# Loading q and k of the first four groups as eight tokens per row, and transposing them by quarter products

## The chip, the cores and the metric

The kernel runs on one core of one Trainium2 chip. The metric is the device time of one launch in microseconds; each figure of a kernel is the median of several runs. TensorE (PE in the profile, PEld for its weight loads) multiplies matrices into PSUM; VectorE (DVE), ScalarE (ACT) and GpSimd (POOL) do the work in between, POOL without PSUM. SyncE (SP) issues all DMAs of this kernel, in the order of its one queue.

## What is computed

Attention within chunks of 64 tokens, then two feed-forward layers on 4608 tokens of width 512. The inputs q, k, v are 8 x 8 x 576 x 64 (batch, head, token, dimension) in float32; the weights come as float64.

```python
scores = matmul(q_c, k_c.transpose(0, 1, 2, 4, 3)) / sqrt(64)     # by chunks of 64 tokens
attn = exp(scores - max(scores)); attn = attn / (sum(attn) + 1e-9)
x = matmul(attn, v_c)                          # -> x: 4608 tokens x 512
h = x @ w_in;  x = relu(h)**2 @ w_out          # 512 -> 2048 -> 512
h = x @ w_in2                                  # second layer
P = a[0] + a[1]*h + a[2]*h**2 + a[3]*h**3
Q = 1 + |b[0]|*|h| + |b[1]|*h**2
out = (P / (Q + 1e-6)) @ w_out2
```

## The kernel before

The work is cut into 36 tiles of 128 tokens and 9 blocks of 512. Products of the two layers are made in three matmuls each, of a high and a low float32r half of both operands (mm3, lines 265 to 269). A block takes 16 steps s: mm_h makes 128 columns of h, act1 squares and splits them, mm_out1 adds them into four accumulators. While the first layer of block b runs, DVE, ACT and POOL make the attention of later tiles, and the weights of the first layer are loaded, made into float32 and split: w_load (DMA), w_words (two instructions on ACT), w_join (DVE), w_split (a cast, then a subtraction on POOL that gives the low half).

The order is written out by hand. Each step is put at a time by `at`, with a correction from the table MOVED; ON says which engine does a copy, a cast or a norm, or how many dummy transposes of the identity (warm) stand at a place. `issue` sorts by time, and the program order of every engine follows from it. So the tables set the order of instructions and not a start: an instruction starts when its engine reaches it and its semaphores allow it.

The change is about block 0, whose 512 tokens are handled as four groups g: 256 tokens of four heads each. For a group, load_group loads q, k or v (tiles qs, ks: two buffers each, by the group's parity; v0, v1, vx0, vx1), g_tr transposes q or k on PE (steps tq, tk), g_copy brings the result from PSUM to SBUF (qc, kc). Then come the scores g_s (step s), max, sub, exp, sum, norm, the transposition of the result g_f (f), its copy (cp), the product with v (pv) and the split of x into two halves (xh, xl). The list `order` in line 819 holds these steps together with words, join and split of the first two weights and the first six half products (half000 is step 0, tokens 0 to 255, first half of the sum). The loads before them stand in the list of line 791. Tiles 4 and 5 follow as whole tiles (tr_second, line 427; mm_s, line 452; f_tr, line 650), and later tiles come by another path with DVE transposes.

In the loop of g_tr a 128 x 128 piece holds 128 tokens of two heads, so a group's q takes four transpositions, and head 2p+h of the group stands in partition half h of column block p:

Of the kernel before, what the change touches and what calls it, by code (L numbers as in the profile page):

```python
# [9 lines left out]
F32 = mybir.dt.float32  # L10
# [13 lines left out]
LN_SHIFT = 20  # L24
ON = {
# [12 lines left out]
MOVED = {  # L38
# [37 lines left out]


@with_exitstack
def attn_moe_moe_kernel(
# [25 lines left out]
    nc = tc.nc  # L105
    B, H, S, D = q.shape
# [16 lines left out]
    h_p = ctx.enter_context(tc.tile_pool(name="hps", bufs=2, space=PSUM))  # L123
# [15 lines left out]
    P = {}  # L139
    T = {}  # L140
# [31 lines left out]
    def tl(pool, shape, dt, nm, tag=None):  # L172
        return P[pool].tile(shape, dt, name=nm, tag=tag or nm)

    def copy(eng, o, x):
        if eng is nc.scalar:
            nc.scalar.activation(out=o, in_=x, func=ACTF.Copy)  # L177
        else:
            eng.tensor_copy(out=o, in_=x)  # L179
# [204 lines left out]
    def half(i):  # L384
        return slice(64 * i, 64 * i + 64)
# [151 lines left out]

    def load_group(g, nm):
        i, k = divmod(g, 2)
        x = tl("attn", [128, 2, 4, D], F32, nm, f"{nm}s{g % 2}" if nm != "v" else f"v{g}" if g < 2 else f"vx{g - 2}")  # L540
        for t in range(2):
            t0 = 256 * i + 128 * t
            nc.sync.dma_start(  # L543
                out=x[:, t], in_={"q": q, "k": k_in, "v": v}[nm][0, 4 * k:4 * k + 4, t0:t0 + 128, :].rearrange("h r d -> r h d"))
        T[nm, "group", g] = x

    def g_tr(g, nm):
        x = T.pop((nm, "group", g))
        ps = h_p.tile([128, 2, 2, 128], F32, name="h", tag="h")
        for p in range(2):  # L550
            for t in range(2):
                nc.tensor.transpose(out=ps[:, p, t], in_=x[:, t, 2 * p:2 * p + 2].rearrange("r h d -> r (h d)"),
                                    identity=P["ident"])
        T[nm, g, "ps"] = ps

    def g_copy(g, nm, eng):
        x = T[nm, g] = tl("attn", [128, 2, 256], F32, nm)
        copy(eng, x.rearrange("d p (t r) -> d p t r", t=2), T.pop((nm, g, "ps")))

    def g_s(g):  # L560
        stage("s0", g, 0)
# [52 lines left out]
    def g_pv(g):  # L614
        stage("softmax", g, 7)
        v_, a = T.pop(("v", "group", g)), T.pop(("a", g))
        o = banks(T["aps", g], 1).rearrange("d c (p t) i -> d c p t i", p=2)
        for t in range(2):
            for p in range(2):
                for c, h in QUARTERS:  # L620
                    nc.tensor.matmul(out=o[half(h), c, p, t], lhsT=v_[half(c), t, 2 * p + h], rhs=a[half(c), t, p, half(h)],
                                     start=True, stop=True)
        T["x", g] = o.rearrange("d c p t i -> d c p (t i)")

# [163 lines left out]
        else:  # L788
            load_tok(t, {"q": q, "k": k_in}[nm], nm + "n", f"{nm}s{t % 2}")

    for i, x in enumerate("k0 q0 v0 q1 k1 w0 q2 k2 q3 w1 k3 v2 v1 w3 w2 w4 k4 v3 w5 q4 k5 q5".split()):
        at(-90 + i, load_nat, x)
    w_keys = [(0, f, half_) for _, f, half_ in w_order]

    def first(x):
# [19 lines left out]
        else:  # L815
            {"max": g_max, "sub": g_sub, "exp": g_exp, "sum": g_sum, "f": g_f, "cp": g_cp, "pv": g_pv,
             "xr": g_raw, "xh": g_hi, "xl": g_lo}[nm](int(t))

    order = """w0 tk0 tq0 qc0 kc0 w1 s0 max0 tq1 sub0 qc1 tk1 exp0 w4 w5 kc1 sum0 s1 tq2 w2 max1 norm0 sub1 exp1 w3 tk2 f0 qc2
               kc2 sum1 cp0 s2 norm1 pv0 max2 xr0 xh0 words0 tq3 sub2 f1 exp2 cp1 xl0 qc3 tk3 words1 pv1 join0  # L820
               split0 kc3 s3 xr1 xh1 sum2 xl1 max3 norm2 join1 split1 half000 sub3 exp3 f2 cp2 sum3 half100 pv2
               norm3 half101 xr2 xh2 xl2 f3 half001 cp3 w7 w8 w9 pv3 xr3 xh3 half010 w10 xl3 w6 half110"""
    for i, x in enumerate(order.split()):
        at(-20 + 0.1 * i, first, x)

# [38 lines left out]
    for t in range(NAT, NTILE + 1, 2):  # L864
        b, i = divmod(t, TPB)
# [140 lines left out]
```

## Time and profile before

| | us |
| --- | --- |
| median of three runs | 1645.58 |
| the three runs | 1642.66, 1645.58, 1646.14 |
| the profiled execution | 1643.19 |
| its span, first to last instruction | 1641.4 |
| PE busy in it | 1630.4 |
| DVE, ACT, POOL busy | 1106.4, 924.8, 355.7 |

The page of the profile is one execution. Busy times of PE are of pipelined matmuls, so two that follow each other overlap by their tail: the distance from one start to the next is what a matmul costs PE. In a timeline a row is a run of equal instructions; in square brackets stands how long the engine was idle before it and who ended that. A DMA row of SP is its issue, not the transfer.

### The profile page before, as it was taken

To read this page: it belongs to the slowest core of one execution; us is meant where nothing else is said; L and a number is where in the kernel's file an instruction comes from. 1 tells how busy PE (TensorE), PEld (TensorE's weight loads), DVE (VectorE), ACT (ScalarE), POOL (GpSimd) and SP (SyncE) were. 2 spreads that over 40 slices of the span, in tenths; PEclk is the share of its full clock that TensorE was granted. 3 is DMA by queue.
4 is the path that set the end of the run, shared out by engine and by line. 5 is a ranking of instruction groups with operands and counts; after the bars stand their busy time and mean duration, and the time that the engine had idled before them with its cause. 6 is when DMAs were issued, how large, how long until landed. Compare 5 with 4: busy or idle time off the path is not lost.

```text
span 1641.4 us, 24428 instructions
## 1 busy us (share of the span) xinstructions
PE 1630.4 (99%) x9357; PEld 1349.6 (82%) x9357; DVE 1106.4 (67%) x1800; ACT 924.8 (56%) x1493; POOL 355.7 (22%) x287
## 2 busy tenths in 40 slices
PE   8999999999999999999999999999999999999999
PEld 7878888888888888888888888888888888888887
DVE  6986666666555565651029787777777777877777
ACT  5863333333333333322457777777777777777776
POOL 3630000000000000000773232323232232323222
PEclk9999999999999999999999999999999999999999
DMA  9754343433434243302321000000010101010000
GB/s 262 211 141 112 80 103 80 114 76 81 102 87 120 69 103 75 84 14 71 96 89 53 26 27 26 26 23 30 1 52 1 52 0 52 1 52 0 3 24 26
DMA packets 218012, 108.56 MB, mean 66 GB/s; under 512 B 186920, under 2 KB 187176, under 8 KB 216744
## 3 DMA queue, kind: packets, MB, share of 16 engines
q1 hardware_dynamic: 217896, 107.02, 24.4%
q8 instruction: 73, 1.20, 0.3%
q14 instruction: 43, 0.35, 0.1%
HBM read 79.69 MB, written 27.26 MB: 65 GB/s over the span
## 4 chain that ended last, share of the span: by engine, by line
PE 97%; DVE 1%; DMA 1%; SPq 0%; ACT 0%; issue 0%; POOL 0%; DVEq 0%; POOLq 0%; ACTq 0%
PE acc L267 16%; PE acc L268 16%; PE acc L269 16%; PE h L267 16%; PE h L268 16%; PE h L269 16%; PE h L473 1%; PE a L452 1%; DMA st<-in_moe_w_out_dram 0%; DMA st<-in_moe_w_in_dram 0%; SPq L543 0%; PE a L304 0%; DVE wc L223 0%; PE a L569 0%; DVE e L524 0%
## 5 line engine op out<-in xcount | busy, mean ns | idle before, releaser
L267 PE MATMUL h<-x,w 128*128 128x512 f32 (+1 forms) x1160 | 450.6, 388 | 0.1
L268 PE MATMUL h<-x,w 128*128 128x512 f32 (+1 forms) x1160 | 449.7, 388 | 0.3 <-DVE x L182 0.3
L269 PE MATMUL h<-x,w 128*128 128x512 f32 (+1 forms) x1160 | 449.6, 388 | 0.0
L182 POOL TENSOR_TENSOR gl<-g,gh 128x512 fp32r<-128x512 f32 x141 | 181.6, 1288 | 533.2 <-ACT gh L177 533.1
L372 ACT ACTIVATE r<-h 128x512 f32<-128x512 f32 x144 | 86.0, 597 | 340.4 <-PE h L269 245.1
L267 PEld LDWEIGHTS h<-x,w 128*128 128x128 f32 x1160 | 217.8, 188 | 45.0 <-POOL w L182 0.3
L268 PEld LDWEIGHTS h<-x,w 128*128 128x128 f32 x1160 | 217.8, 188 | 44.9 <-DVE x L182 0.5
L269 PEld LDWEIGHTS h<-x,w 128*128 128x128 f32 x1160 | 217.9, 188 | 44.6
L179 DVE CAST gh<-r 128x512 fp32r<-128x512 f32 x135 | 59.6, 442 | 268.5 <-ACT r L373 258.1
L267 PE MATMUL acc<-gh,w 128*128 128x512 f32 x576 | 226.5, 393 | 0.0
L268 PE MATMUL acc<-gl,w 128*128 128x512 f32 x576 | 224.4, 390 | 0.0
L269 PE MATMUL acc<-gh,w 128*128 128x512 f32 x576 | 224.3, 389 | 0.0
L267 PE MATMUL acc<-w,gl 128*128 128x512 f32 x575 | 223.7, 389 | 0.0
L269 PE MATMUL acc<-w,gh 128*128 128x512 f32 x575 | 223.7, 389 | 0.0
L268 PE MATMUL acc<-w,gh 128*128 128x512 f32 x575 | 223.7, 389 | 0.0
L704 DVE SCALAR_TENSOR_TENSOR t<-h,co,t 128x512 f32<-128x512 f32 (+1 forms) x145 | 123.3, 851 | 147.8 <-ACT t L703 147.3
L182 POOL TENSOR_TENSOR gl<-r,gh 128x512 fp32r<-128x512 f32 x21 | 27.3, 1299 | 598.7 <-ACT gh L177 480.6
L177 ACT ACTIVATE gh<-g 128x512 fp32r<-128x512 f32 x141 | 88.7, 629 | 81.4 <-DVE g L735 81.4
L267 PEld LDWEIGHTS acc<-gh,w 128*128 128x128 f32 x576 | 108.1, 188 | 24.2 <-DVE ev L179 0.9
L702 ACT ACTIVATE h<-h 128x512 f32<-128x512 f32 (+1 forms) x145 | 86.3, 595 | 72.2 <-PE h L269 71.9
L269 PEld LDWEIGHTS acc<-gh,w 128*128 128x128 f32 x576 | 108.2, 188 | 22.7
L267 PEld LDWEIGHTS acc<-w,gl 128*128 128x128 f32 x575 | 108.0, 188 | 22.7 <-POOL gl L182 0.2
(114 smaller groups left out, 2294.2 us busy)
## 6 DMA issues: line engine op xcount, KB each, us to landing
st<-in_moe_w_in_dram SPq DMA_DIRECT2D x32, 512.0 KB, 5.1
st<-in_moe_w_out_dram SPq DMA_DIRECT2D x32, 512.0 KB, 4.0
x2d<-ev SPq DMA_DIRECT2D x36, 256.0 KB, 3.5
x<-x2d SPq DMA_DIRECT2D x9, 1024.0 KB, 4.7
out_dram<-ev SPq DMA_DIRECT2D x35, 256.0 KB, 2.0
w2d<-wc SPq DMA_DIRECT2D x32, 256.0 KB, 2.1
w<-w2d SPq DMA_DIRECT2D x32, 256.0 KB, 2.7
v<-in_v_dram SPq DMA_DIRECT2D x28, 256.0 KB, 4.5
```

The costliest lines, as they stand in the source:

```text
L177: nc.scalar.activation(out=o, in_=x, func=ACTF.Copy)
L179: eng.tensor_copy(out=o, in_=x)
L182: eng.tensor_tensor(out=o, in0=x, in1=hi.bitcast(F32), op=ALU.subtract)
L267: nc.tensor.matmul(out=o, lhsT=al, rhs=bh, start=first and i == 0, stop=False)
L268: nc.tensor.matmul(out=o, lhsT=ah, rhs=bl, start=False, stop=False)
L269: nc.tensor.matmul(out=o, lhsT=ah, rhs=bh, start=False, stop=last and i == len(pairs) - 1)
L372: nc.scalar.activation(out=r, in_=ps, func=ACTF.Relu)
L452: nc.tensor.matmul(out=o[half(c), h, p], lhsT=q_[half(h), p, half(c)], rhs=k_[half(h), p, half(c)], start=True, stop=True)
L473: nc.tensor.matmul(out=o[c][half(h), i, p], lhsT=v_[half(c), 2 * p + h], rhs=a_[h][half(c), p] if t < 2 * TPB else a_[h][half(c), :, p], s ...
L702: nc.scalar.activation(out=h2, in_=ps, func=ACTF.Square)
L704: nc.vector.scalar_tensor_tensor(out=t, in0=h2, scalar=co[:, 5:6], in1=t, op0=ALU.mult, op1=ALU.add)
```

## The change

load_group takes q and k in one DMA instead of two: the four heads' 256 tokens go to 128 partitions, 32 of a head, and a partition holds eight tokens in a row (j), 2 KB that stand together in memory. Before, a partition held one token of four heads for each of two halves, in pieces of 256 B. v is loaded as before. g_tr makes sixteen products of 64 x 64 with the identity: for each j, partitions 0 to 63 (two heads) and 64 to 127 (the other two). The result stands by j in PSUM, and g_copy sets the tokens back in order while it copies: it reads every 64th element, eight at a time. Head 2h+p now stands in half h of block p, so g_pv takes `a[half(c), t, h, half(p)]`.

Besides, the tables ON and MOVED, the list of loads and the list `order` are new. In ON, among others, qc0 and qc1 go from DVE to ACT, kc2 from DVE to ACT and qc2 from ACT to DVE, norm0 from POOL to DVE, norm1 from DVE to POOL, norm5 from DVE to POOL, the casts split16 and split28 from DVE to ACT, gc2 and the copy of q of tile 5 from ACT to DVE. Of the dummies, warm0 goes from 15 to 16, warm2 from 5 to 1, warm3 from 1 to 0, warm10 from 0 to 4. MOVED shifts loads, words, joins and splits of the first layer's weights up to the start of block 1 by fractions of a step; two of its lines:

```diff
-    "w_load:0,7,1": -0.802, "load_qk:0,qs,3": 1.2, "f_copy:4,0,1": -0.15, "w_words:(0,6,0)": 0.149,
+    "load_qk:0,qs,3": 0.475, "f_copy:4,0,1": -0.15, "load_qk:0,ks,1": 0.499, "act1:3": -0.001,
```

```diff
@@ -537,25 +543,34 @@
 
     def load_group(g, nm):
         i, k = divmod(g, 2)
-        x = tl("attn", [128, 2, 4, D], F32, nm, f"{nm}s{g % 2}" if nm != "v" else f"v{g}" if g < 2 else f"vx{g - 2}")
+        if nm != "v":
+            x = tl("attn", [128, 8, D], F32, nm, f"{nm}s{g % 2}")
+            if True:
+                nc.sync.dma_start(
+                    out=x.rearrange("r j d -> r (j d)"),
+                    in_={"q": q, "k": k_in}[nm][0, 4 * k:4 * k + 4, 256 * i:256 * i + 256, :]
+                    .rearrange("a (o j) d -> a o (j d)", j=8))
+            T[nm, "group", g] = x
+            return
+        x = tl("attn", [128, 2, 4, D], F32, nm, f"v{g}" if g < 2 else f"vx{g - 2}")
         for t in range(2):
             t0 = 256 * i + 128 * t
             nc.sync.dma_start(
-                out=x[:, t], in_={"q": q, "k": k_in, "v": v}[nm][0, 4 * k:4 * k + 4, t0:t0 + 128, :].rearrange("h r d -> r h d"))
+                out=x[:, t], in_=v[0, 4 * k:4 * k + 4, t0:t0 + 128, :].rearrange("h r d -> r h d"))
         T[nm, "group", g] = x
 
     def g_tr(g, nm):
         x = T.pop((nm, "group", g))
-        ps = h_p.tile([128, 2, 2, 128], F32, name="h", tag="h")
-        for p in range(2):
-            for t in range(2):
-                nc.tensor.transpose(out=ps[:, p, t], in_=x[:, t, 2 * p:2 * p + 2].rearrange("r h d -> r (h d)"),
-                                    identity=P["ident"])
+        ps = h_p.tile([128, 8, 64], F32, name="h", tag="h")
+        for j in range(8):
+            for a in range(2):
+                nc.tensor.matmul(out=ps[half(a), j], lhsT=x[half(a), j], rhs=P["ident"][half(a), half(a)],
+                                 start=True, stop=True)
         T[nm, g, "ps"] = ps
 
     def g_copy(g, nm, eng):
         x = T[nm, g] = tl("attn", [128, 2, 256], F32, nm)
-        copy(eng, x.rearrange("d p (t r) -> d p t r", t=2), T.pop((nm, g, "ps")))
+        copy(eng, x.rearrange("d b (o j) -> d b o j", j=8), T.pop((nm, g, "ps")).rearrange("d j (b o) -> d b o j", b=2))
 
     def g_s(g):
         stage("s0", g, 0)
@@ -618,7 +633,7 @@
         for t in range(2):
             for p in range(2):
                 for c, h in QUARTERS:
-                    nc.tensor.matmul(out=o[half(h), c, p, t], lhsT=v_[half(c), t, 2 * p + h], rhs=a[half(c), t, p, half(h)],
+                    nc.tensor.matmul(out=o[half(h), c, p, t], lhsT=v_[half(c), t, 2 * p + h], rhs=a[half(c), t, h, half(p)],
                                      start=True, stop=True)
         T["x", g] = o.rearrange("d c p t i -> d c p (t i)")
 
@@ -788,7 +803,7 @@
         else:
             load_tok(t, {"q": q, "k": k_in}[nm], nm + "n", f"{nm}s{t % 2}")
 
-    for i, x in enumerate("k0 q0 v0 q1 k1 w0 q2 k2 q3 w1 k3 v2 v1 w3 w2 w4 k4 v3 w5 q4 k5 q5".split()):
+    for i, x in enumerate("k0 q0 q1 w3 v1 v0 k1 w0 q2 k2 k3 q3 w1 v2 k4 w2 w4 v3 w5 q4 k5 q5".split()):
         at(-90 + i, load_nat, x)
     w_keys = [(0, f, half_) for _, f, half_ in w_order]
 
@@ -816,10 +831,10 @@
             {"max": g_max, "sub": g_sub, "exp": g_exp, "sum": g_sum, "f": g_f, "cp": g_cp, "pv": g_pv,
              "xr": g_raw, "xh": g_hi, "xl": g_lo}[nm](int(t))
 
-    order = """w0 tk0 tq0 qc0 kc0 w1 s0 max0 tq1 sub0 qc1 tk1 exp0 w4 w5 kc1 sum0 s1 tq2 w2 max1 norm0 sub1 exp1 w3 tk2 f0 qc2
-               kc2 sum1 cp0 s2 norm1 pv0 max2 xr0 xh0 words0 tq3 sub2 f1 exp2 cp1 xl0 qc3 tk3 words1 pv1 join0
-               split0 kc3 s3 xr1 xh1 sum2 xl1 max3 norm2 join1 split1 half000 sub3 exp3 f2 cp2 sum3 half100 pv2
-               norm3 half101 xr2 xh2 xl2 f3 half001 cp3 w7 w8 w9 pv3 xr3 xh3 half010 w10 xl3 w6 half110"""
+    order = """w0 tk0 tq0 w1 kc0 qc0 s0 max0 tq1 sub0 qc1 tk1 exp0 w4 w5 sum0 norm0 kc1 s1 tq2 max1 xr0 sub1 exp1 w3 tk2 f0 qc2
+               kc2 sum1 cp0 w2 words0 norm1 s2 pv0 xh0 tk3 max2 sub2 f1 exp2 tq3 cp1 xr1 join0 pv1 qc3 xl0 xh1
+               words1 split0 kc3 s3 sum2 xl1 max3 norm2 xr2 half000 join1 split1 sub3 w6 exp3 f2 cp2 half100
+               sum3 pv2 norm3 xh2 half101 xl2 f3 half001 cp3 w7 w8 w9 pv3 xr3 xh3 half010 w10 xl3 half110"""
     for i, x in enumerate(order.split()):
         at(-20 + 0.1 * i, first, x)
```

PE's first instructions before, from the first dummies to the transposition of the third group; h is a PSUM tile for a transposition or a product, a one for scores, s the line of the operation:

```order
L304 MATMUL a<-ident 128x128 x15
L552 MATMUL h<-ident,k 128x128 x4
L552 MATMUL h<-ident,q 128x128 x4
L304 MATMUL a<-ident 128x128 x5
L569 MATMUL a<-k,q 64x64 x16
L552 MATMUL h<-ident,q 128x128 x4
L552 MATMUL h<-ident,k 128x128 x4
L304 MATMUL a<-ident 128x128 x8
L569 MATMUL a<-k,q 64x64 x16
L552 MATMUL h<-ident,q 128x128 x4
L304 MATMUL a<-ident 128x128 x6
L552 MATMUL h<-ident,k 128x128 x4
```

and in the changed kernel:

```order
L310 MATMUL a<-ident 128x128 x16
L567 MATMUL h<-ident,k 64x64 x16
L567 MATMUL h<-ident,q 64x64 x16
L310 MATMUL a<-ident 128x128 x5
L584 MATMUL a<-k,q 64x64 x16
L567 MATMUL h<-ident,q 64x64 x16
L567 MATMUL h<-ident,k 64x64 x16
L310 MATMUL a<-ident 128x128 x8
L584 MATMUL a<-k,q 64x64 x16
L567 MATMUL h<-ident,q 64x64 x16
L567 MATMUL h<-ident,k 64x64 x16
L621 MATMUL a<-ident,e 128x128 x4
```

The transpositions keep their places up to the second scores, and after these both of the third group stand side by side ahead of the first f (L621), with one dummy behind it in the place of six ahead.

SP's first loads before (st is a weight, k, q and v are the groups'):

```order
L543 DMA k<-in_k_dram 128x4x64 x2
L543 DMA q<-in_q_dram 128x4x64 x2
L543 DMA v<-in_v_dram 128x4x64 x2
L543 DMA q<-in_q_dram 128x4x64 x2
L543 DMA k<-in_k_dram 128x4x64 x2
L204 DMA st<-in_moe_w_in_dram 128x2x512
L543 DMA q<-in_q_dram 128x4x64 x2
L543 DMA k<-in_k_dram 128x4x64 x2
L543 DMA q<-in_q_dram 128x4x64 x2
L204 DMA st<-in_moe_w_in_dram 128x2x512
L543 DMA k<-in_k_dram 128x4x64 x2
L543 DMA v<-in_v_dram 128x4x64 x4
```

and in the changed kernel, where an x2 on q or k is two groups and not two halves of one:

```order
L549 DMA k<-in_k_dram 128x1x512
L549 DMA q<-in_q_dram 128x1x512 x2
L210 DMA st<-in_moe_w_in_dram 128x2x512
L558 DMA v<-in_v_dram 128x4x64 x4
L549 DMA k<-in_k_dram 128x1x512
L210 DMA st<-in_moe_w_in_dram 128x2x512
L549 DMA q<-in_q_dram 128x1x512
L549 DMA k<-in_k_dram 128x1x512 x2
L549 DMA q<-in_q_dram 128x1x512
L210 DMA st<-in_moe_w_in_dram 128x2x512
L558 DMA v<-in_v_dram 128x4x64 x2
L404 DMA kn<-in_k_dram 64x8x64 x2
```

A weight and both halves of two groups' v moved ahead of the second k, and the third k and fourth k stand together.

ACT's first instructions before (k, q and at are copies out of PSUM, e the exponentials, x the high half of x):

```order
L177 ACTIVATE k<-h 128x512
L586 ACTIVATE e<-e 128x512
L177 ACTIVATE k<-h 128x512
L586 ACTIVATE e<-e 128x512
L177 ACTIVATE q<-h 128x512
L177 ACTIVATE at<-a 128x512
L177 ACTIVATE x_69<-a 128x2x2x128
```

and in the changed kernel:

```order
L183 ACTIVATE k<-h 128x512
L183 ACTIVATE q<-h 128x512 x2
L601 ACTIVATE e<-e 128x512
L183 ACTIVATE k<-h 128x512
L601 ACTIVATE e<-e 128x512
L183 ACTIVATE k<-h 128x512
L183 ACTIVATE at<-a 128x512
```

Two copies of q that stood on DVE now stand ahead of the first exponential.

## Rows read from the trace of the kernel before

**Rows 1.** Page: engines' busy time (share, instructions); part 4, shares of the chain.

```profile
PE 1630.4 (99%) x9357; PEld 1349.6 (82%) x9357; DVE 1106.4 (67%) x1800; ACT 924.8 (56%) x1493; POOL 355.7 (22%) x287
...
PE 97%; DVE 1%; DMA 1%; SPq 0%; ACT 0%; issue 0%; POOL 0%; DVEq 0%; POOLq 0%; ACTq 0%
```

**Rows 2.** Waits of PE, 0 to 110 us: us in total, times, longest.

```profile
PE a L621 <- DMA v<-in_v_dram: 1.1, 1, 1.1
PE h L650 <- DVE ah L179: 0.8, 1, 0.8
PE h L650 <- POOL e L524: 0.7, 1, 0.7
...
PE a L606 <- POOL e L598: 0.2, 1, 0.2
```

**Rows 3.** Timeline, TensorE's first steps: start, us, engine, line, operation, tiles, count.

```profile
1.36 3.46 PE L304 MATMUL a<-ident 128*128 128x128 f32 x15 [1.36 <-POOL ident masks.py:199]
...
4.62 1.06 PE L552 MATMUL h<-ident,k 128*128 128x128 f32 x4
...
5.47 0.76 PE L552 MATMUL h<-ident,q 128*128 128x128 f32 x4
...
7.10 1.15 PE L569 MATMUL a<-k,q 64*64 64x64 f32 x32 [0.33 <-DVE q L179]
...
8.18 0.66 PE L552 MATMUL h<-ident,q 128*128 128x128 f32 x4
...
11.99 0.66 PE L552 MATMUL h<-ident,q 128*128 128x128 f32 x4
...
12.48 0.82 PE L304 MATMUL a<-ident 128*128 128x128 f32 x6
...
20.32 1.10 PE L569 MATMUL a<-k,q 64*64 64x64 f32 x32
```

**Rows 4.** Timeline of PE around the first steps of tile 4.

```profile
30.86 0.63 PE L427 MATMUL a<-ident,qn 128*128 128x128 f32 x4
...
33.29 0.69 PE L452 MATMUL a<-k,q 64*64 64x64 f32 x32
33.91 0.50 PE L267 MATMUL h<-x,w 128*128 128x512 f32 x1
```

**Rows 5.** Timeline, ACT in the first steps.

```profile
9.74 0.63 ACT L586 ACTIVATE e<-e 128x512 f32<-128x512 f32 x1 [3.43 <-DVE e L582]
10.28 0.58 ACT L177 ACTIVATE k<-h 128x512 f32<-128x512 f32 x1
...
17.48 0.67 ACT L217 ACTIVATE st<-st 128x512 int32<-128x512 uint32 x1
```

**Rows 6.** DMA view of 0 to 40 us, 1 us a figure; page, part 6.

```profile
GB/s 0 14 201 205 216 239 220 221 224 341 282 226 230 277 339 249 183 158 172 304 377 391 387 267 164 217 331 287 175 184 233 219 368 412 369 367 375 391 404 333
...
k<-in_k_dram SPq DMA_DIRECT2D x8, 128.0 KB, 3.5
...
w<-w2d SPq DMA_DIRECT2D x32, 256.0 KB, 2.7
```

**Rows 7.** Windows of 20 us: busy (instructions) by engine, granted clock, DMA share, GB/s.

```profile
0.00:20.00 20.00, 16.01 (x218) 14.05 (x218) 11.06 (x20) 8.18 (x14) 2.71 (x9) 1.00 0.95 215
...
60.00:80.00 20.00, 20.00 (x150) 16.39 (x150) 17.36 (x25) 15.05 (x28) 14.40 (x12) 1.00 0.80 238
80.00:100.00 20.00, 19.18 (x118) 15.49 (x117) 18.98 (x33) 11.98 (x21) 8.98 (x7) 1.00 0.56 133
```

**Rows 8.** Chain that ended last, 26 to 48 us: start, us, what.

```profile
28.95 6.40 DMA st<-in_moe_w_in_dram
```

**Rows 9.** Timelines of DVE and POOL, 30 to 56 us.

```profile
36.74 1.79 DVE L223 SCALAR_TENSOR_TENSOR wc<-wc,st 128x512 int32<-128x512 int32 x1 [1.84 <-ACT st L217]
...
45.89 0.68 DVE L223 SCALAR_TENSOR_TENSOR wc<-wc,st 128x512 int32<-128x512 int32 x1
...
36.70 1.29 POOL L182 TENSOR_TENSOR w<-wc,w 128x512 fp32r<-128x512 f32 x1
```

90 rows, old and new, of tables (MOVED, ON) are left out of this document.

## The prediction

> **What bounds the kernel now.** I read the page first, then the waits of PE, then the first 34 us step by step. The page's busy line and chain give the frame: PE is busy for 1630.4 of 1641.4 us and holds 97% of the chain that ended last [rows 1]. Nothing but PE's own work and PE's holes can move the end. The holes are early, and the waits name them [rows 2]: besides the 1.36 us before its first instruction [rows 3] nine short ones up to 31 us, 1.1 us for v the longest, 0.2 the shortest; after that only 0.7 us behind POOL's e and 0.8 us behind DVE's ah. Busy time before 31 us also hides filler: 15 + 5 + 8 + 6 dummy transposes of the identity that warm does.
>
> So I work out two numbers: when PE reaches the transposes of tile 4 (L427, 30.86 us now [rows 4]), which I call the entry and from which PE runs on its own work, and what becomes of the two later waits. A kernel of 1645 us can be told from no change at about 0.2%, 3.3 us; the whole stake here is of that size.
>
> **The loads.** Eight loads of 256 KB change from 1024 pieces of 256 B to 128 of 2 KB. From the third us to the fortieth data flow without a gap; with mostly 256 B pieces (third to ninth us) the row gives 201 to 239 GB/s, mean 218; with weight rows (last eight us) about 377 [rows 6]. So 256 KB cost 1.20 us now and some 0.70 us then; the same shape from another source (w<-w2d, 256 KB in 2 KB rows) lands 2.7 us after its issue on an emptier queue, against 3.5 us for half as many bytes of k here [rows 6]. The saving is 8 x 0.50 = 4.0 us of DMA time (bounds 0 and 4.4), and eight issues fewer on SP. Not all of it arrives: k of group 3 goes into the buffer of group 1 and is issued behind that group's transposition, which comes later than now (below), and q3, w1 and v2 stand behind it in SP's queue. I take 2 to 3 us for the weights that follow. Nothing before 31 us waits for weights on PE now, so this is worth only what DMA waits cost: the 1.1 us for v, whose loads of group 1 move from the thirteenth place to the fifth.
>
> **The transposition.** A group's q or k cost four matmuls of 128x128, 0.49 us from 11.99 to 12.48 [rows 3]. Now it is sixteen of 64x64, alternating between the two diagonal quarters of the array. The scores of a group (L569) are sixteen of that shape in that alternation (two passes each, so x32): 7.10 to 8.18, 1.08 us [rows 3]. The scores of tile 4 (L452) are the same count over all four quarters in turn: 33.29 to 33.91, 0.62 us [rows 4]. The alternation is the former, so I take 1.08, with 0.62 as the lower end: 0.59 us more each, 8 x 0.59 = 4.7 us of PE work (1.0 at the lower end), all ahead of the last scores. Of the six dummies behind s1 one is left, 0.5 us back; the sixteenth in front costs 0.2; four new ones stand behind half010, 0.4 us, where PE has to wait for x of the third group from DVE in any case.
>
> The copies out of PSUM now read every 64th element. No row has that; the nearest are a plain copy, 0.58 us on ACT, and the words, at every second element, 0.67 [rows 5]. I take no change, with 0.09 us each as the upper end; four of the eight lie on the path, 0.4 us.
>
> **The chain to the entry, before -> after.** First transposition: PE's dummies stand 0.217 us apart at first ((4.62 - 1.36) / 15) and four transpositions took 0.85 us from 4.62 to 5.47 but 0.49 at 11.99 [rows 3]; that is the lower of the two clock levels, 1.2 GHz, until some 5.5 us, with dummies and transpositions back to back before it rose, though the granted clock reads 1.00 in every window [rows 7]. Sixteen of them end at 4.83, so k's earlier landing buys nothing: 4.62 -> 4.83. At the lower level 1.08 is 2.16; until 5.5 a third is done, the rest takes 0.75: q's transposition 5.47 -> 6.25, ended 7.33. Its copy now stands on ACT, 0.15 + 0.58 us: first scores (s0) 7.10 -> 8.1.
> From s0 to s1: the first exponential starts 2.64 us behind s0 (7.10 to 9.74) [rows 3, 5], which would be 10.7. But ACT must first take qc1, and tq1 ends at 8.1 + 2 x 1.08 = 10.3, so qc1 is done at 11.0; exp0 and kc1 follow as now (9.74 to 10.86, 1.12 us [rows 5]): s1 at 12.2.
> From s1 to s2: three blocks of 1.08 on PE (s1, tq2, tk2) end at 15.4, the copy kc2 on ACT 0.15 + 0.58: s2 at 16.2.
> From s2 to s3: s2 1.08, pv0 by the row of sixteen over four quarters 0.62, tk3 1.08, f1 by the old four transposes 0.49, tq3 1.08, its copy 0.73; 5.1 in all: s3 20.32 [rows 3] -> 21.3. The old wait of 1.1 us for v lies in this stretch and falls away.
> Behind s3 the steps and engines are nearly the old ones, so I carry it on: **the entry comes 1.0 us later**, 31.9. With the four-quarter price in the same chain it comes 0.3 us earlier; with the strided copies dear 1.4 later.
>
> **The later waits.** The 0.7 us at 43.9 hang on a weight load: the chain goes from its landing at 35.35 over ACT, DVE's join, the softmax of tile 4 and POOL's e to PE [rows 2, 8]. With that landing 2 to 3 us earlier and PE 1.0 later the wait goes whole: -0.7. The 0.8 us behind DVE's ah lie in the window 80:100, where DVE works 18.98 of 20 us [rows 7]; PE comes there 0.3 us later than before, and DVE loses one norm to POOL (norm5) but gets the copy of q of tile 5. I take half: -0.4. Bounds for both together: -1.5, and +3.3 as the slow rival has it.
>
> **Sum.** +1.0 - 0.7 - 0.4 = -0.1 us. The profiled execution took 1643.19 us, so 1643.1 by it; the median of the three runs, 1645.58, lies 2.4 above, and they span 3.5 us. I predict on the median: **1645.5**.
>
> **Rivals.**
> *DVE behind POOL (slow).* A DVE instruction that reads and writes SBUF stands still while POOL works: the join at 36.74 took 1.79 us with POOL busy from 36.70 to 37.99, where an undisturbed one takes 0.68 [rows 9]; 1.1 us a meeting. DVE has 2.64 and 1.02 us free in the windows 60:80 and 80:100 [rows 7]. The change puts norm5 on POOL and reorders joins, casts and gh on DVE there. Once the meetings eat that slack, each costs PE its 1.1: three are 3.3 us, no later wait is saved but the first: 1645.6 + 1.0 - 0.7 + 3.3 = 1649.2. For it: both windows are nearly full. Against: ACT takes two weight casts from DVE (split16, split28; gc2 goes the other way), and the weights come earlier. The Trainium skill (SBUF — State Buffer, "SBUF: two separate sides") calls the pair of ports an exclusive lock, held for the whole instruction; by that rule, too, nothing is shared in such a meeting, and the rows agree.
> *The loads decide (fast).* If the early chain is really carried by the full DMA queue, all 4.0 us come through, with the 0.2 of filler lost: 1641.8. For it: the queue has no gap until 40 us, and PE's longest wait is for v. Against: eight of the nine short waits before 31 us are for ACT, DVE or POOL [rows 2], and the chain above closes without a DMA.
> *The quarters overlap.* With 0.62 the entry is 0.3 us early, and with the waits -1.1: 1645.6 - 1.4 = 1644.2. For it: L452 does it with the same shape; against: not in this alternation. The Trainium skill (TensorEngine Tiling (Array Packing), "Key Properties") says that different tiles of the array load and multiply in parallel; by that an estimate for two quarters would be about 0.43 us for sixteen, no dearer than the old four. The trace does not agree: L569 takes 1.08 for two quarters.
> That the change doesn't do what it says: the pieces could reach the queue no longer than before; then v's earlier place alone is left, and the first wait stays: 1645.6 + 1.0 - 0.4 = 1646.2, inside the range.
>
> **How the numbers follow.** Forecast and its neighbours 0.60; DVE behind POOL 0.16; the loads decide 0.14; the quarters overlap 0.10. The bounds of the sum are -1.8 (entry -0.3, both waits gone) and +1.4 (entry +1.4, no wait gone) around 1645.6; the runs shown scatter by 1.8 us on either side of their middle. Together that is the range 1642.0 to 1648.8; it holds the forecast and the overlap whole, and of the outer two the half that falls short of its price. Faster by over 0.2% (below 1642.3): the fast rival and a trace of the forecast's edge, 0.16. Slower (above 1648.9): the slow rival's larger part, 0.13. Within: 0.71.
>
> **What would show it.** In the trace after: sixteen quarter products 1.08 us apart from the next block (else the overlap); s0 near 8.1, s1 12.2, s2 16.2, s3 21.3, the transposes of tile 4 near 31.9; no wait of PE for v; no wait before tile 4's f_tr; the sixth weight load landing near 33 instead of 35.35. Wrong it would be if s0 stands at 7.1 or earlier (then the copies or k's landing, not PE, set it), or if PE shows more than 1 us of waits between 45 and 110.

## The result, and the profile after

The changed kernel takes 1661.3 us (median of four runs, 1660.71 to 1662.37), the kernel before 1644.46 in the same comparison. The ratio is 1.0106, with a 95% interval of 1.0094 to 1.0119. That is about 17 us slower, where 1645.5 was forecast with 1648.8 as the upper end.

The page of the kernel after, busy line and chain, beside [rows 1]:

```profile
PE 1639.5 (99%) x9581; PEld 1357.5 (82%) x9581; DVE 1098.8 (66%) x1793; ACT 927.4 (56%) x1499; POOL 357.5 (22%) x288
...
PE 95%; DMA 3%; SPq 1%; DVE 0%; POOL 0%; issue 0%; ACT 0%; DVEq 0%; ACTq 0%
```

The span went from 1641.4 to 1658.6 us. PE is busy for 9.1 us more and idle for 8.1 us more. The chain now holds 3% of DMA instead of 1%. The waits of PE from 0 to 120 us (us in total, times, longest) say which, beside [rows 2]:

```profile
PE h L567 <- DMA k<-in_k_dram: 6.1, 3, 3.3
PE h L567 <- DMA q<-in_q_dram: 3.0, 2, 2.1
PE acc L273 <- POOL w L188: 1.7, 1, 1.7
PE h L273 <- POOL w L188: 1.4, 3, 1.0
```

The transposition (now L567) waits 9.1 us for q and k; before, it waited for neither. The wait for v is gone, as foretold. Two waits for weights from POOL are new. The timeline of PE's first steps (start, us, line, count, idle time before) shows where, beside [rows 3]:

```profile
1.36 3.68 PE L310 MATMUL a<-ident 128*128 128x128 f32 x16 [1.36 <-POOL ident masks.py:199]
7.23 1.15 PE L567 MATMUL h<-ident,k 64*64 64x64 f32 x32 [2.19 <-DMA k<-in_k_dram]
10.44 1.98 PE L567 MATMUL h<-ident,q 64*64 64x64 f32 x32 [2.06 <-DMA q<-in_q_dram]
...
13.60 1.97 PE L584 MATMUL a<-k,q 64*64 64x64 f32 x32
15.36 1.39 PE L567 MATMUL h<-ident,q 64*64 64x64 f32 x32
20.05 1.97 PE L567 MATMUL h<-ident,k 64*64 64x64 f32 x32 [3.31 <-DMA k<-in_k_dram]
...
27.55 1.15 PE L567 MATMUL h<-ident,k 64*64 64x64 f32 x32 [0.56 <-DMA k<-in_k_dram]
28.63 0.66 PE L621 MATMUL a<-ident,e 128*128 128x128 f32 x4
```

The first k is used at 7.23 us instead of 4.62, the first scores stand at 13.60 instead of 7.10, and the entry (transposes of tile 4) at 46.06 instead of 30.86 [rows 4]. Of the 17.2 us of span 15.2 are lost by then. The DMA view of 0 to 40 us, 1 us a figure (busy tenths of the 16 engines, then GB/s), beside [rows 6]:

```profile
DMA  0002489872263635972222226999422367399999
GB/s 0 0 18 76 113 274 252 161 178 86 98 176 114 177 85 85 301 209 88 100 102 98 96 98 147 276 248 216 105 102 96 129 150 190 67 149 239 369 366 303
```

Where only q and k are under way (18 to 23 us) the queue moves some 100 GB/s and the 16 engines are busy for 2 tenths. From 19 to 22 us it is a share of 0.26 at 100 GB/s: as much as 4 engines of 16 would show, 25 GB/s each. In [rows 6] the microseconds from 18 to 23 read 172 to 391 GB/s. At 100 GB/s a load of 256 KB takes 2.6 us; the prediction's price was 0.70.

### The profile page after: what moved, and what is told of

The parts are those of the page before. It is cut to its first block, busy times and chain, and to the rows that moved or that the text cites. A ratio compares the mean times of both kernels' runs of the same rounds, so it can differ in the third digit from the quotient of the medians.

```text
span 1658.6 us, 24864 instructions
## 1 busy us (share of the span) xinstructions
PE 1639.5 (99%) x9581; PEld 1357.5 (82%) x9581; DVE 1098.8 (66%) x1793; ACT 927.4 (56%) x1499; POOL 357.5 (22%) x288
## 4 chain that ended last, share of the span: by engine, by line
PE 95%; DMA 3%; SPq 1%; DVE 0%; POOL 0%; issue 0%; ACT 0%; DVEq 0%; ACTq 0%
PE acc L273 16%; PE acc L274 15%; PE acc L275 15%; PE h L274 15%; PE h L275 15%; PE h L273 15%; DMA st<-in_moe_w_out_dram 1%; PE h L479 1%; PE a L458 1%; DMA k<-in_k_dram 1%; SPq L558 1%; DMA st<-in_moe_w_in_dram 0%; DMA qs<-in_q_dram 0%; SPq L549 0%; SPq L210 0%; POOL w L188 0%
## 5 line engine op out<-in xcount | busy, mean ns | idle before, releaser
L274 PEld LDWEIGHTS acc<-w,gh 128*128 128x128 f32 x575 | 108.0, 188 | 22.4
```

Of the source, the lines that this page charges most:

```text
L274: nc.tensor.matmul(out=o, lhsT=ah, rhs=bl, start=False, stop=False)
```

## The experiments

Theory A: the outermost dimension of the new load's source is 4 (heads), and the load runs on 4 of the 16 DMA engines. B: TensorE's clock, which fell to its lower level while PE waited, makes a good part of the loss. C: the quarter products and the strided copies cost more than thought. E: the new order is the loss, by its first steps (E1) or its tables (E2). The kernels after_... are the changed kernel with something altered or taken back, the kernels before_... the kernel before with something put in; inter_k1 and old_k1 go back to after_inter and after_old. Each kernel was compared with the kernel before on its own chip (medians 1643.7 to 1643.9 us).

| kernel | loads, products | order, tables | median, us | ratio [95%] |
| --- | --- | --- | --- | --- |
| after_inter | 32 rows outermost | new | 1648.86 | 1.0035 [1.0022, 1.0047] |
| before_one | as changed | old | 1657.79 | 1.0083 [1.0070, 1.0097] |
| after_old | as before | new | 1647.43 | 1.0022 [1.0013, 1.0031] |
| before_inter | 32 rows outermost | old | 1645.86 | 1.0016 [1.0007, 1.0025] |
| after_four | as changed, a DMA per head | new | 1653.71 | 1.0065 [1.0052, 1.0077] |
| after_pair | as changed, a DMA per two heads | new | 1682.15 | 1.0234 [1.0220, 1.0248] |
| after_warm | as changed | new, more dummies | 1661.00 | 1.0105 [1.0091, 1.0119] |
| inter_k1 | as after_inter | new, k1 earlier | 1652.71 | 1.0047 [1.0034, 1.0061] |
| before_first | as before | new first steps alone | 1645.60 | 1.0008 [1.0000, 1.0017] |
| before_tables | as before | new tables alone | 1647.91 | 1.0025 [1.0015, 1.0034] |
| old_k1 | as before | new, k1 earlier | 1648.53 | 1.0026 [1.0016, 1.0037] |
| before_twice | whole transposes twice | old | 1644.38 | 1.0001 [0.9992, 1.0010] |

**The outermost dimension.**

```diff
# after_inter
-                    .rearrange("a (o j) d -> a o (j d)", j=8))
+                    .rearrange("a (o j) d -> o a (j d)", j=8))
# g_copy
-        copy(eng, x.rearrange("d b (o j) -> d b o j", j=8), ....rearrange("d j (b o) -> d b o j", b=2))
+        copy(eng, x.rearrange("d a (o j) -> d a o j", j=8), ....rearrange("d j (o a) -> d a o j", a=4))
# g_s: the halves of the array are now the halves of the tokens
-                    for h in range(2):
-                        ... lhsT=q_[half(h), p, j], rhs=k_[half(h), p, j]
+                for t, h in QUARTERS:
+                    ... lhsT=q_[half(t), 2 * p + h, j], rhs=k_[half(t), 2 * p + h, j]
```

> The changed kernel with one thing different in the q/k loads of the first four groups: still one transfer of 256 KB in rows of 2 KB, but with the 32 rows per head as the outermost dimension of the source and the 4 heads inside it, so partition 4o+a holds head a. The products that follow keep their number (sixteen quarter transposes a load, 32 quarter products for the scores) and read other columns; order and tables stay. Theory A (a load whose outermost dimension is 4 runs on 4 of the 16 DMA engines, and the first steps wait for it): the first k lands some 3 us sooner, the DMA rate in a stretch of q/k loads rises from about 100 to over 200 GB/s, PE's waits for k and q fall from 9.1 us to under 2 us, the first scores are at 9 us or earlier instead of 13.6 us, and the time falls to 1644 to 1649 us (ratio to before 1.000 to 1.003). Rival C (the sixteen quarter products and the copies that read PSUM with a stride are the loss): they are all still there, so 1658 to 1662 us. Rival E (the other order of the first steps is the loss): also 1655 us or more, with the waits for k and q gone but other waits in their place.

Bytes, row length, number of products and order are those of the changed kernel, and 12.4 us of its 17.5 (1661.3 against the 1643.8 of before here) are gone. Not all of that need be the load: the score products now go over all four quarters of the array, and a group's scores take 0.52 us (7.60 to 8.12 below) instead of 1.08, an estimated 4 x 0.57 = 2.3 us less PE work. Its DMA view (0 to 40 us) and PE's first steps:

```profile
DMA  0079889999998400898967889999999479899999
GB/s 0 0 172 375 164 276 329 298 170 226 315 393 258 170 16 0 221 332 256 282 176 165 154 257 401 378 279 362 287 170 154 69 151 190 283 406 324 289 346 414
```

```profile
4.82 1.15 PE L567 MATMUL h<-ident,k 64*64 64x64 f32 x32
...
7.60 0.69 PE L583 MATMUL a<-k,q 64*64 64x64 f32 x32
8.12 1.10 PE L567 MATMUL h<-ident,q 64*64 64x64 f32 x32
12.71 1.97 PE L567 MATMUL h<-ident,k 64*64 64x64 f32 x32 [3.50 <-DMA k<-in_k_dram]
```

Stretches of 2 tenths and 100 GB/s are gone, the first k waits for nothing, the first scores stand at 7.60 us. One wait stays, 3.5 us for k1, so "under 2 us" was wrong; it belongs to the order (below).

before_one has the changed load_group, g_tr, g_copy, g_s and g_pv in the kernel before; before_inter the same with the edits above.

> The kernel before with its own order and tables, and only the pieces of the change: q and k of the first four groups in one transfer each with 4 heads outermost, sixteen quarter transposes, the strided copies. Theory A: k and q wait on 4 DMA engines here too; all eight loads stand ahead of the early weights in the queue, so 1655 to 1668 us (ratio 1.006 to 1.014). Rival E (the new order alone is the loss): 1644 to 1649 us. Rival C: 1649 to 1662 us, but with PE's waits for k and q under 2 us.

> The kernel before with its own order and tables, with the 256 KB loads in rows of 2 KB whose source has 32 rows outermost and 4 heads inside (as in after_inter), sixteen quarter transposes and strided copies. Theory A: the loads run on all 16 engines and land no later than before; the quarter products add 8 x 0.59 = 4.7 us of PE work, which may be hidden in part behind the steps' own chain: 1642 to 1650 us. Rival C: 1650 us or more, with no waits for k and q.

In the old order the same step, one to inter, is worth 11.9 us. Waits of PE in before_one, 0 to 120 us:

```profile
PE h L561 <- DMA k<-in_k_dram: 4.1, 3, 2.2
PE h L561 <- DMA q<-in_q_dram: 2.5, 2, 1.8
```

before_inter shows no such wait and lies 2.1 us above before. So A holds in both orders, and C is left with those 2.1 us and what the cheaper scores hide, up to 2.3. To be sure that it is the load and not the other places of the heads or the other quarters of the scores, two kernels keep everything in SBUF and all products word for word and cut the load along the heads:

```diff
# after_four (four heads a in turn, 32 rows outermost)
-                    out=x.rearrange("r j d -> r (j d)"), in_=...[0, 4 * k:4 * k + 4, ...].rearrange("a (o j) d -> a o (j d)", j=8)
+                    out=x[32 * a:32 * a + 32]..., in_=...[0, 4 * k + a, ...].rearrange("(o j) d -> o (j d)", j=8)
# after_pair (two pairs b in turn, 2 heads outermost)
+                    out=x[64 * b:64 * b + 64]..., in_=...[0, 4 * k + 2 * b:4 * k + 2 * b + 2, ...].rearrange("a (o j) d -> a o (j d)", j=8)
```

> The changed kernel with each q/k load of 256 KB cut into four transfers of 64 KB, one for each head (32 rows of 2 KB outermost). What lies in SBUF, the products, the copies, the order and the tables stay word for word. Theory A (4 heads outermost put a load on 4 of the 16 DMA engines): the loads run on 16 engines as in after_inter, the first k's products start by 5.5 us instead of 7.2, PE's waits for k and q fall from 9.1 to under 5 us (k1's place in the queue stays), 1646 to 1652 us; SP issues 32 transfers instead of 8, at about 0.5 us each, which may cost 1 to 2 us of that. Rival (what helped in after_inter was the other arrangement of heads in SBUF and the score products on other quarters, not the load): 1658 us or more.

> The changed kernel with each q/k load cut into two transfers of 128 KB, two heads outermost in each, into the same places; everything else as in the changed kernel. Theory A: the number of DMA engines follows the outermost dimension, so 2 engines instead of 4. A stretch of q/k loads alone moves about 50 GB/s instead of 100 (2.6 us more for each 256 KB, 21 us for the eight), the first k lands some 2 us later, PE's waits for k and q grow from 9.1 us to 20 to 35 us, and the time to 1670 to 1690 us. Rival (one transfer of 256 KB is slow because it is one transfer): two smaller ones land sooner, 1661 us or less.

With two heads outermost the time rises by 20.9 us to 1682.15. DMA view and PE's waits of after_pair (0 to 40 us; 0 to 130 us):

```profile
DMA  0001111111149955111255217921111111112111
GB/s 0 0 14 23 47 49 49 49 49 49 49 102 283 236 121 139 49 47 49 69 155 139 63 28 183 309 78 49 49 49 51 49 49 49 49 49 66 49 47 49
```

```profile
PE h L567 <- DMA k<-in_k_dram: 16.5, 7, 5.3
PE h L567 <- DMA q<-in_q_dram: 8.5, 5, 3.5
```

Half the rate, 49 GB/s, at half the busy share (0.13 from 28 to 36 us): the rate of a load goes with its outermost dimension, 2 or 4, and smaller transfers do not help by being smaller. after_four, with the products of the changed kernel, gains 7.6 us, less than after_inter and 1.7 us outside its own range. Its first k is used at 4.96 us, but SP now issues 32 transfers, and from 2 to 7 us they move 142 GB/s: 64 KB for each 0.45 us that SP takes to issue one. So k1 comes later, and PE waits 4.0 us for it. The load alone is thus worth at least 7.6 us; by after_inter it is an estimated 10.1 (12.4 less the cheaper scores) to 12.4.

The Trainium skill (DMA: Bandwidth & Descriptors, "Why a DMA increments its semaphore by 16 and not by 1") has the rule: a transfer gets the largest number of engines, at most 16, that divides the slowest dimension over 1 of both sides. By it 4 heads give 4 engines, 2 heads 2, 32 rows 16; the rates of 100 and 49 GB/s and the busy tenths of 2 and 1 agree. It spoke against this change before it ran, and was not weighed.

**The clock.** after_warm adds dummies where PE waits:

```diff
-w0 tk0 tq0 ...  "warm0": 16
+w0 tk0 w20 tq0 ... w21 tk1 ... w22 tk2   "warm0": 34, "warm20": 14, "warm21": 22, "warm22": 4
```

> The changed kernel with more of its dummy transposes where PE waits for k and q: 34 instead of 16 ahead of the first k, 14 new ones between k0 and q0, 22 ahead of k1, 4 ahead of k2. They compute nothing that is used. Theory B (a good part of the 16 us is the lower clock of TensorE after each wait): the granted clock stays at 1.00 in 10 to 30 us instead of 0.67, the first score products take 1.1 us instead of 1.97, 1652 to 1657 us. Theory A alone (the loads set the time, the clock is a by-product): the same clock, but the products then wait longer for the next load, 1658 to 1662 us.

Windows of 10 us on PE (busy, instructions, granted clock, DMA share, GB/s), first the changed kernel, then after_warm:

```profile
10.00:20.00 10.00, 6.31 (x101) 0.67 0.50 143
20.00:30.00 10.00, 9.29 (x158) 0.69 0.56 149
```

```profile
10.00:20.00 10.00, 6.85 (x127) 0.99 0.51 141
20.00:30.00 10.00, 8.14 (x150) 0.84 0.57 146
```

The clock comes back, in full until 20 us and in part (0.84) behind it, and the time does not move (1661.0 against 1661.3). PE in after_warm still waits until 20.10 us for k1 (20.05 in the changed kernel), and its last scores stand at 35.49 (35.41). B falls: the lower level was paid out of time in which PE had nothing to do.

**What is left: 5.1 us of after_inter over before.** after_old takes the loads, g_tr, g_copy, g_s and g_pv of before into the new order:

> The changed kernel's order and tables with the loads, transposes, copies and products of the kernel before (two transfers of 128 KB per load, four whole transposes). Theory A and rival C: the loss is gone, 1642 to 1649 us (ratio 0.998 to 1.003). Rival E: the loss stays, 1655 us or more.

It is 3.6 us slower than before; the order is a second, smaller loss, and the new pieces of after_inter add 1.4 to it, with intervals that overlap. It shows PE waiting 3.4 us for k1, which the new list puts behind w3, v1 and v0, 1 MB. inter_k1 and old_k1 move k1 ahead of them:

```diff
-"k0 q0 q1 w3 v1 v0 k1 w0 q2 ...
+"k0 q0 q1 k1 w3 v1 v0 w0 q2 ...
```

> after_inter with one entry of the load list moved: k1 ahead of w3, v1 and v0 (it stood behind these 1 MB). Theory E1 (what the new order of the first steps costs, 3.0 to 3.7 us, is k1's late place in the queue): PE's wait of 3.5 us for k1 is gone, the second scores are at about 12.5 us instead of 16.5, 1644.5 to 1647 us (ratio 1.000 to 1.002). Rival E2 (the cost of the new order lies in the later tables, as in PE's wait of 1.7 us for GpSimd's split of a weight after 60 us): 1648 to 1650 us, with the wait for k1 gone and the time given back before 70 us.

> after_old (the order and tables of the change with the loads and transposes of before) with k1 ahead of w3, v1 and v0 in the load list. With whole transposes PE issues fewer instructions than in inter_k1, where a stop of 3.1 us with no releaser in the first value product took the gain. Theory E1: the wait of 3.4 us for k1 goes, no such stop comes, and the time falls from 1647.4 to 1643 to 1646 us. Rival: what stands ahead of k1 now stands behind it, and the next load or the tables take the time, 1646.5 to 1649 us.

In both the wait for k1 is gone and nothing is won: q2 is late instead (2.1 and 1.9 us), and in inter_k1 PE also stops for 3.1 us with no releaser (the profile shows nothing that it waits for). inter_k1 is 3.9 us slower than after_inter, outside both of its ranges; old_k1 lies in the rival's. E1 in this form falls. The two halves of the order apart (before_first: the list, the string `order` and the counts of dummies; before_tables: ON and MOVED):

> The kernel before with three things from the change: the load list (k0 q0 q1 w3 v1 v0 k1 ...), the order of the first steps, and the numbers of dummy transposes that belong to it. Loads, transposes, products and the two tables stay as before. The new order as a whole, with its tables, costs 3.0 to 3.7 us. Theory E1 (its first steps cost it): 1646 to 1649 us, with PE waiting over 3 us for k1. Rival E2 (its tables cost it, by late weights after 60 us): 1643 to 1645 us.

> The kernel before with the two tables of the change (which engine takes which copy and split, and the shifts of due times), its own load list, order of the first steps and numbers of dummies. Theory E2: the loss of the new order is here, 1646 to 1649 us, with PE's wait of 1.7 us for GpSimd's split of a weight between 60 and 80 us. Theory E1: 1643 to 1645 us.

The tables alone cost 4.0 us, as E2 had it; the first steps alone 1.7 (interval from 0), between the two ranges, with a wait of 3.7 us for k1; both together 3.6. By the medians the prices do not add, but the intervals are too wide to be sure. Part of the tables' price comes early: the entry of before_tables stands at 32.62 us instead of 30.86, with 1.9 us of PE waits for copies of k on ACT. Waits of PE in before_tables, 60 to 200 us, and POOL's timeline there, then the same gl in the kernel before:

```profile
PE acc L273 <- POOL w L188: 1.6, 1, 1.6
PE h L273 <- POOL w L188: 1.3, 2, 1.1
```

```profile
59.38 1.29 POOL L188 TENSOR_TENSOR gl<-r,gh 128x512 fp32r<-128x512 f32 x1 [7.10 <-ACT gh L183]
60.62 1.27 POOL L188 TENSOR_TENSOR w<-wc,w 128x512 fp32r<-128x512 f32 x1
61.83 0.62 POOL L185 CAST w<-wc 128x512 fp32r<-128x512 f32 x1
62.53 1.29 POOL L188 TENSOR_TENSOR w<-wc,w 128x512 fp32r<-128x512 f32 x1
```

```profile
52.15 1.45 POOL L182 TENSOR_TENSOR gl<-r,gh 128x512 fp32r<-128x512 f32 x1 [0.25 <-ACT gh L177]
```

POOL stands for 7.10 us at the head of its queue before a gl whose gh ACT has not made, and the weight's split stands behind it; PE at 61.95 waits 1.08 us for that split. The longest wait, 1.65 us at 67.19, is for a later split, before which POOL waited 1.59 us for a cast on ACT. ACT itself stands in front of the words of a weight whose load has not landed, with gh behind them (waits of ACT in before_tables, 44 to 76 us):

```profile
ACT wc L221 <- DMA st<-in_moe_w_out_dram: 5.0, 1, 5.0
```

The changed kernel has both (ACT waits 4.74 us for such a load, POOL 6.94 us until 72.30 for the same gl), and after_old and after_inter show the wait of ACT with 3.0 and 3.1 us; in before and before_first ACT waits for no load there. That this chain is the whole price of the tables was not tried.

**PE time in the first steps.**

```diff
-                nc.tensor.transpose(out=ps[:, p, t], ...)
+                for _ in range(2):
+                    nc.tensor.transpose(out=ps[:, p, t], ...)
```

> The kernel before with every transpose of a q/k load issued twice into the same place (8 whole transposes a load instead of 4), to price PE time in these steps by itself: 32 more transposes, 8 x 0.49 = 3.9 us of PE work against the 8 x 0.59 = 4.7 us that the quarter products add. Theory of the prediction (the first steps wait on one another, most of such work lies in PE's idle time there): 1644 to 1646 us. Rival (all of it on the path): 1647 to 1648 us.

3.9 us more work on PE moves the time by 0.5 us, with no change inside its interval (1.6 us at most). It is not all hidden: the entry stands at 33.08 us instead of 30.86, 0.9 us of it a wait for q of tile 4. before_inter has less to hide, an estimated 4.7 - 2.3 = 2.4 us with its cheaper scores, so PE work alone is not likely to make its 2.1 us. What before_inter has and before_twice has not is a stop of 2.0 us with no releaser in the last scores:

```profile
PE a L577 <- issue: 2.0, 1, 2.0
```

What would remove this stop was not tried.

## Why the prediction was wrong

**The loads: the step that failed.** "256 KB cost 1.20 us now and some 0.70 us then", with w<-w2d as "the same shape from another source". It has the same bytes and the same row length, but w<-w2d has 128 rows outermost and this load 4 heads. At 100 GB/s a load cost 2.6 us, not 0.70; the term was to bring 4.0 us of DMA time (bounds 0 and 4.4, nothing below zero), and the source with 4 heads outermost cost 7.6 us (after_four) to 12.4 (after_inter). What row length alone is worth stays open: with 32 outermost the view of after_inter shows 375 GB/s from 3 to 4 us, but 172 and 164 on either side, 237 on the mean of the three against 207 in [rows 6], and neither after_inter nor before_inter is faster than before. "k's earlier landing buys nothing: 4.62 -> 4.83" was argued for a k that lands early; none of the bounds had one that lands at 7.2.

**The chain.** By the start of the scores and the entry, us:

| | s0 | s1 | s2 | s3 | entry |
| --- | --- | --- | --- | --- | --- |
| before | 7.10 | 10.91 | 14.72 | 20.32 | 30.86 |
| forecast | 8.1 | 12.2 | 16.2 | 21.3 | 31.9 |
| changed kernel | 13.60 | 23.85 | 29.50 | 35.41 | 46.06 |
| after_inter | 7.60 | 16.52 | 20.64 | 25.70 | 37.29 |
| before_inter | 8.79 | 12.29 | 16.89 | 21.84 | 34.28 |

With wide loads and the old order the chain stands within 0.7 us of the forecast up to s3; most of the rest is the stop in s3. That is in part luck: the forecast was made for the new order and for scores of 1.08 us, and here they take 0.5. What the forecast missed in the new order is k1: v was seen to move from the thirteenth place to the fifth, but not that k1 then stands behind 1 MB. At the 218 to 377 GB/s of [rows 6] this is an estimated 2.8 to 4.8 us, and after_inter and after_old show waits of 3.5 and 3.4. That moving k1 back alone wins nothing, inter_k1 and old_k1 show. The forecast carried what the entry loses on to the end in full, and gave the new order no loss of its own; after_old prices it at 3.6 us.

**The transposition.** Sixteen quarter products take 1.08 us (27.55 to 28.63 in the changed kernel) and not 0.62: right. That 4.7 us of PE work would move the entry by 1.0 only was not tested by itself; before_twice, with 3.9 us of other work in the same places, moves it by 2.2 and the time by 0.5.

**The copies.** "No change": right. Two of the changed kernel's copies, on ACT and on DVE, against 0.58 and 0.69 of plain ones:

```profile
8.43 0.60 ACT L183 ACTIVATE k<-h 128x512 f32<-128x512 f32 x1 [6.41 <-PE h L567]
...
27.20 0.68 DVE L185 COPY q<-h 128x512 f32<-128x512 f32 x1
```

**The later waits.** -1.1 was forecast; the wait for DVE's ah and that for POOL's e did go, but 3.1 us for weights from POOL came in place of their 1.5. The sign "more than 1 us of waits between 45 and 110" was the right one to name.

**The rivals.** The slow one named POOL, but by meetings with DVE, three of 1.1 us; what showed is POOL's own queue, standing for ACT. The loads as a gain fell: after_inter and before_inter have the fast loads and are no faster than before. The overlap of quarters fell by the 1.08. That "the pieces could reach the queue no longer than before" was near the right question and took the wrong side: by the rates and busy shares the loads run on fewer engines.

## What to carry to other kernels

Before pricing a DMA by its bytes and row length, read its outermost dimension on both sides: a comparison row is the same shape only if that agrees too. An einops pattern decides it without changing a byte ("a o" against "o a": 7.6 to 12.4 us here). And a list of loads is one queue: for each entry that moves forward, sum the bytes that now stand ahead of the one needed next.

## What the runs showed of the hardware

**A narrow load holds up the queue behind it.** SP's issues in the changed kernel and then in after_inter (start, us, transfer, count):

```profile
3.63 8.53 SPq L558 DMA_DIRECT2D v<-in_v_dram  x4
12.20 2.14 SPq L549 DMA_DIRECT2D k<-in_k_dram  x1
```

```profile
3.39 2.11 SPq L558 DMA_DIRECT2D v<-in_v_dram  x4
5.54 2.85 SPq L549 DMA_DIRECT2D k<-in_k_dram  x1
```

The four issues for v, themselves of 128 rows, take 8.53 us instead of 2.11 while a weight and three of the narrow loads stand ahead (the three are 768 KB, 7.9 us at 100 GB/s). So k1 was issued 6.7 us later, and from 9 to 16 us the changed kernel's view above has the 16 engines busy for 2 to 6 tenths only.

**PE stops that no engine releases.** Stops with no releaser of 0.8 to 3.1 us appear in the kernels with quarter products and wide loads (before_inter 2.0, after_inter 0.3 and 1.4, after_four 0.8, inter_k1 3.1), each in the first value product or in the last scores. Each time a 16 KB packet of the instruction queue stands 2.4 to 3.1 us ahead of the end of the stop: at 21.5 us in before_inter (PE goes on at 24.35), 25.25 in after_inter (27.71), 26.0 in after_four (28.96), 19.25 in inter_k1 (22.36). The quarter of a microsecond from 25.25 in after_inter, DMA view:

```profile
q8 instruction: 1, 0.02, 27.5%
```

The changed kernel, whose DMA engines are less full, shows none, and other such packets (29.75 in after_inter, 26.0 in before_inter) have no stop behind them. That PE waits for its instructions is argued from the times alone; no run tried it.
